# Regrouping PSUM for batches three to eight: three double and two single banks, attention in four pieces, relus over two banks

## The chip, the cores and the metric

One core of one Trainium2 chip. The metric is the device time of one execution in microseconds, median of several runs; all runs told here were in the fast state or, where there was one run only, of unknown state. The length of one batch inside the trace is from the first matmul of its first layer to the same matmul of the next batch.

## The reference

```python
k_proj = einsum('ks,bhsd->bhkd', E, k); v_proj = einsum('ks,bhsd->bhkd', F, v)
attn = softmax(q @ k_proj^T / 8)                 # 8 batches, 8 heads, 1024 rows, 64 wide
x = (attn @ v_proj) as 8192 x 512
out = relu(x @ w_in)**2 @ w_out                  # 512 -> 2048 -> 512
```

## The kernel before

Each batch has two chunks of 512 rows. A chunk is a first layer (16 groups of four 128x512 matmuls, emptied by relu on ScalarE and squared on VectorE) and a second layer (seven products by Strassen's scheme instead of eight, accumulated in ps_x, ps_y and ps_z). First-layer groups go in pairs: pair k has two halves, n = 0 and 1, that share one buffer of relus and are squared together. From the second batch on, steps are numbered 0 to 61: 0-15 and 31-46 are first-layer groups, 16-30 and 47-61 parts of products. Attention of the next batch is slipped in ahead of numbered steps: scores (q times k_proj), their exponentials, the sums of these and their reciprocals, values (exponentials times v_proj), and normalize (values times reciprocals). "Project" makes k_proj and v_proj. FFN matmuls use TensorE as one array of 128 x 128 ("128*128" in a profile line), scores and values as smaller tiles ("64*64", "64*32"). One turn from FFN matmuls to attention and back is called an excursion below, and the 0.216 us of one 512-column matmul, or of a set of tiles that runs at once (four scores, eight values), a slot. The program orders each engine by hand.

```python
aps = ...tile_pool(name="aps", bufs=2, space=PSUM)   # attention: 2 buffers of two banks
fps = ...tile_pool(name="fps", bufs=4, space=PSUM)   # FFN: 4 single banks, in turn

PIECES = {                                           # attention of the next batch, by step
    1: "copy_kp", 2: "copy_vp", 4: "copy_v_down",
    20: "scores 0, scores 1, exponentials 0", 21: "exponentials 1",
    23: "sums 0, values 0 0, reciprocals 0", 25: "normalize 0 0",
    28: "scores 2, scores 3, exponentials 2", 29: "exponentials 3",
    47: "values 0 1, sums 1, reciprocals 1", 48: "normalize 0 1",
    53: "values 1 0, values 1 1", 54: "normalize 1 0", 55: "normalize 1 1",
}                                                    # and "project" of the batch after at 53

def square(k, n, ps):                                # pair k, half n
    ...
    nc.scalar.activation(r[:, n], ps[:], AF.Relu)    # one relu per bank of 512 columns
    ...                                              # after n == 1: hsq = r * r on VectorE

second = [p1a, p2a, p1b, p1c] + lohi(p5) + lohi(p6) + lohi(p3) + lohi(p7) + [p2b]
second += [p4_last] if last else lohi(p4)
# p1, p6, p7, p4 accumulate into ps_y (read out after each); p5, p3 into ps_z; p2 into ps_x
```

The softmax here doesn't subtract the row's maximum and nothing guards it: scores larger than these inputs give would overflow.

Of the kernel before, what the change touches and what calls it, by code (L numbers as in the profile page):

```python
# [8 lines left out]
P = 128  # L9
F32 = mybir.dt.float32  # L10
BF16 = mybir.dt.bfloat16
AF = mybir.ActivationFunctionType
# [8 lines left out]
def kernel(  # L21
# [42 lines left out]
    sum_pool = ctx.enter_context(tc.tile_pool(name="sums", bufs=1))  # L64
    part_pool = ctx.enter_context(tc.tile_pool(name="part", bufs=1))
    out_pool = ctx.enter_context(tc.tile_pool(name="outp", bufs=2))
    aps = ctx.enter_context(tc.tile_pool(name="aps", bufs=2, space=bass.MemoryType.PSUM))
    fps = ctx.enter_context(tc.tile_pool(name="fps", bufs=4, space=bass.MemoryType.PSUM))

    def att_psum(shape, dtype):  # L70
        return aps.tile(shape, dtype, tag="att", name="ps_att")

    def ffn_psum(name, shape=(P, 512), dtype=F32):
        return fps.tile(list(shape), dtype, tag="ffn", name=name)

    def rows(src, b):
        return src[b].rearrange("h (p i) d -> p h (i d)", i=NI)
# [83 lines left out]
    class Attention:  # L161
# [9 lines left out]
        def transpose_q(self):  # L171
            nc.sync.dma_start_transpose(out=self.qT[:], in_=self.Q[:].rearrange("p h c -> p (h c)"))

        def project(self):
            ps = self.ps["kv"] = ffn_psum("ps_kv")
            kv = self.K[:].rearrange("p h (i d) -> p h i d", i=NI)
            vv = self.V[:].rearrange("p h (i d) -> p h i d", i=NI)
            for i in range(NI):
                f, l = i == 0, i == NI - 1
                nc.tensor.matmul(ps[0:KP, :], lhsT=ET[:, i, :], rhs=kv[:, :, i, :], start=f, stop=l)  # L180
                nc.tensor.matmul(ps[KP:P, :], lhsT=FT[:, i, :], rhs=vv[:, :, i, :], start=f, stop=l)  # L181
# [10 lines left out]
        def copy_vp(self):  # L192
            self.vp = proj_pool.tile([P, H, 2, D // 2], BF16, name="vp")
            ps = self.ps["kv"]
            ps_v = ps[KP:P, :].rearrange("k (h d e) -> k h e d", h=H, e=2)
            for e in range(2):
                nc.scalar.copy(self.vp[KP:P, :, e], ps_v[:, :, e])
# [209 lines left out]


    PIECES = {
        1: "copy_kp", 2: "copy_vp", 4: "copy_v_down",  # L410
        20: "scores 0, scores 1, exponentials 0", 21: "exponentials 1",
        23: "sums 0, values 0 0, reciprocals 0", 25: "normalize 0 0",
        28: "scores 2, scores 3, exponentials 2", 29: "exponentials 3",
        47: "values 0 1, sums 1, reciprocals 1", 48: "normalize 0 1",
        53: "values 1 0, values 1 1", 54: "normalize 1 0", 55: "normalize 1 1",
    }
    BATCH_1 = {
        33: "project", 34: "copy_kp, transpose_q, copy_vp", 37: "copy_v_down",
        48: "scores 0, scores 1, exponentials 0", 49: "exponentials 1",
        51: "scores 2, scores 3, exponentials 2", 52: "exponentials 3",  # L420
        55: "sums 0, sums 1, logs 0, logs 1, inverses 0", 57: "inverses 1",
# [2 lines left out]
    }  # L424

    BATCH_2 = {
        12: "project", 13: "copy_kp, transpose_q", 14: "copy_vp", 17: "copy_v_down",
        24: "scores 0, scores 1, exponentials 0", 25: "exponentials 1",
        27: "scores 2, scores 3, exponentials 2", 28: "exponentials 3",
        30: "sums 0, sums 1, logs 0", 31: "logs 1", 33: "inverses 0",  # L430
# [20 lines left out]
    def calls(table, n):  # L451
        for c in filter(None, table.get(n, "").split(", ")):
            name, *args = c.split()
            yield name, [int(a) for a in args]

    def ffn_groups(b, xT):
# [30 lines left out]
        def chunk(ch):  # L487
# [17 lines left out]
            def square(k, n, ps):  # L505
                hsq = st["hsq"]
                if n == 0:
                    st["r"] = relu_pool.tile([P, 2, TCH], F32, name="h_relu")
                r = st["r"]
                if (b, ch, k, n) == (0, 0, 0, 1):  # L510
                    nc.vector.tensor_scalar_max(r[:, n], ps[:], 0.0)
                else:
                    nc.scalar.activation(r[:, n], ps[:], AF.Relu)  # L513
                if n == 0:
                    return
                (h, j), (h1, _) = pairs[k]
                o = hsq[:, :, j, :] if h != h1 else hsq[:, h, j:j + 2, :]
                if k in ON_SCALAR.get((b, ch), ()):
                    nc.scalar.activation(o, r[:], AF.Square)
                    return operands_after(k)  # L520
                multiply = lambda: nc.vector.tensor_tensor(out=o, in0=r[:], in1=r[:], op=ALU.mult)  # L521
                if b == 0 and ch == 0 and k in (4, HFB - 1):
                    held.append(multiply)
                    return
                multiply()
                operands_after(k)
# [8 lines left out]
            def operands(q4, which):  # L535
                sums(st["hsq"], st["s"], q4, which)

            def step1(k, n):
                if k == 0 and n == 0:
                    begin()  # L540
                if held:
                    held.pop()()
                h, j = pairs[k][n]
                ps = ffn_psum("ps_h")
                first(ch, HFB * h + j, ps, range(NCB))
                square(k, n, ps)

# [25 lines left out]

            lo, hi = range(0, 4), range(4, 8)

            ALL = slice(0, 2)

            def bank(name):


                if last and name == "ps_y":
                    return [aps.tile([P, MH], F32, tag="att", name=name)[:] for _ in range(2)]
                return [ffn_psum(name)[:].rearrange("p (t m) -> p t m", t=2)]

            def parts(ps):

                return [(ps[0], ALL)] if len(ps) == 1 else [(ps[t], t) for t in range(2)]

            def copy(to, name):
                for ps, t in parts(st[name]):  # L590
                    nc.scalar.copy(to[:, t], ps)  # L591

            def add(to, name, more):
                for ps, t in parts(st[name]):
                    nc.vector.tensor_tensor(out=to[:, t], in0=ps, in1=more[:, t], op=ALU.add)  # L595

            def p1a():
                st["x"], st["y"], st["z"] = (bank(n) for n in ("ps_x", "ps_y", "ps_z"))
                h = st["hsq"]
                st["A11"], st["A12"] = h[:, 0, :, 0:TH], h[:, 1, :, 0:TH]  # L600
                st["A22"] = h[:, 1, :, TH:TCH]
                st["o0"], st["o1"] = (out_pool.tile([P, 2, DM], F32, name="o_sb") for _ in range(2))
                product(st["y"], st["A11"], W11, lo, True)

            def p2a():
                if b:
                    operands(1, (1, 3, 2))
                product(st["x"], st["A12"], W21, lo, True)

            def p1b():  # L610
                product(st["y"], st["A11"], W11, range(4, 7))
# [4 lines left out]
                copy(st["a"], "y")  # L616

            def p5(js):
                product(st["z"], st["s"][0], T1[:], js, js[0] == 0)
                if js[0]:  # L620
                    st["d"] = part_pool.tile([P, 2, MH], F32, name="p_d")
                    copy(st["d"], "z")
# [7 lines left out]
            def p3(js):  # L630
                product(st["z"], st["s"][3], W22, js)
                if js[0]:
                    add(st["o0"][:, :, MH:DM], "z", st["b"])
                    if last:
                        nc.sync.dma_start(out_rows[b, ch, 0, :, :, MH:DM], st["o0"][:, :, MH:DM])

            def p7(js):
                product(st["y"], st["s"][2], T3[:], js)
# [3 lines left out]
                        nc.sync.dma_start(out_rows[b, ch, 1, :, :, MH:DM], st["o1"][:, :, MH:DM])  # L642

            def p2b():
                product(st["x"], st["A12"], W21, hi)
                add(st["o0"][:, :, 0:MH], "x", st["a"])
                s = slice(0, MH if last else DM)
                nc.sync.dma_start(out_rows[b, ch, 0, :, :, s], st["o0"][:, :, s])

            def p4(js):  # L650
                product(st["y"], st["A22"], T4[:], js)
# [8 lines left out]
                    nc.sync.dma_start(out_rows[b, ch, 1, :, tb, 0:MH], st["o1"][:, tb, 0:MH])  # L660

            lohi = lambda p: [lambda: p(lo), lambda: p(hi)]
            second = [p1a, p2a, p1b, p1c] + lohi(p5) + lohi(p6) + lohi(p3) + lohi(p7) + [p2b]
            second += [p4_last] if last else lohi(p4)
            return steps, second, begin_sums, operands

# [20 lines left out]
    with tc.manual_schedule(engines=ORDERED):  # L687
# [11 lines left out]
        for b in range(B):  # L699
            for n, g in enumerate(ffn_groups(b, cur.xT)):  # L700
                if b == 0:
                    for name, args in calls(SECOND_HALF, n):
                        getattr(cur, name)(*args)
                    for name, args in calls(WEIGHTS, n):
                        combine_weights(args[0], name)
                    if n == 31:
                        nxt = load_batch(1)
                if nxt:
                    for name, args in calls((BATCH_1, BATCH_2, PIECES)[min(b, 2)], n):
                        getattr(nxt, name)(*args)  # L710
                    if n == (35, 14, 1)[min(b, 2)]:
                        ahead = load_batch(b + 2)
                    if b and n == 33 and ahead:
                        ahead.transpose_q()
                    if b and n == 53 and ahead:
                        ahead.project()
                g()
            if b == 0:
                nxt.normalize(1, 1)
            cur, nxt, ahead = nxt, ahead, None  # L720


# [28 lines left out]
```

## Time and profile before

| | before |
|---|---|
| median of 3 runs | 483.76 us (483.60 to 484.57) |
| span of the profiled run | 482.4 us |
| TensorE / VectorE / ScalarE busy | 470.3 / 314.1 / 261.5 us |
| a middle batch (third to sixth) | 57.30 us |
| the seventh batch (no projection) | 55.46 us |

### The profile page before, as it was taken

The page shows a single profiled execution, that of the slowest core. Times are in us where ns is not written, and L with a number is a line of the kernel's source. Part 1 is how long each engine was busy: PE and PEld are TensorE (multiplying, and loading weights), DVE is VectorE, ACT ScalarE, POOL GpSimd, SP SyncE. Part 2 cuts the span into 40 slices and gives each one's busy share as a digit, 9 for nine tenths or more (in the row PEclk, how much of TensorE's full clock was granted, in tenths as well). Part 3 has the DMA queues.
Part 4 walks back from the last instruction along what each step waited for, and adds up shares of the span by engine and source line. Part 5 has one row for each costly group of instructions (what it writes and reads, how often), then busy time and mean ns, then how long its engine had stood idle before and what let it go on. Part 6 is the DMA issues. An engine that isn't in the chain of part 4 may idle for free.

```text
span 482.4 us, 8423 instructions
## 1 busy us (share of the span) xinstructions
PE 470.3 (97%) x3630; PEld 292.6 (61%) x3630; DVE 314.1 (65%) x382; ACT 261.5 (54%) x413; POOL 34.7 (7%) x48
## 2 busy tenths in 40 slices
PE   4899999999999999999999999999999999999997
PEld 2544676475574746657475665747557474666656
DVE  1478955554958559493776848667494855948383
ACT  2387544758427564466635667176662756545351
POOL 6540020020020001000010000100000000000000
PEclk9999999999999999999999999999999999999999
DMA  9999989579989086941859147690702102020202
GB/s 155 203 204 207 168 181 200 137 120 229 180 128 229 12 175 88 180 94 50 153 86 227 22 115 131 91 200 1 165 11 75 25 1 88 1 88 0 88 1 87
DMA packets 72789, 55.46 MB, mean 115 GB/s; under 512 B 33968, under 2 KB 64944, under 8 KB 72752
## 3 DMA queue, kind: packets, MB, share of 16 engines
q0 software_dynamic: 30624, 29.36, 39.4%
q1 hardware_dynamic: 42128, 25.56, 21.1%
q8 instruction: 28, 0.46, 0.4%
q14 instruction: 9, 0.07, 0.0%
HBM read 59.24 MB, written 16.78 MB: 158 GB/s over the span
## 4 chain that ended last, share of the span: by engine, by line
PE 92%; DVE 3%; DMA 3%; ACT 1%; POOL 1%; issue 0%; POOLq 0%
PE ps_h L459 44%; PE ps_y L479 23%; PE ps_z L479 11%; PE ps_x L479 6%; DMA V_sb<-in_v_dram 3%; PE ps_kv L180 2%; PE ps_att L221 2%; PE ps_att L206 2%; DVE hsq L521 1%; DVE s L473 1%; PE ps_v L284 0%; DVE xT L246 0%; DVE xT L351 0%; PE ps_kv L181 0%; ACT h_relu L513 0%; POOL K_sb L93 0%
## 5 line engine op out<-in xcount | busy, mean ns | idle before, releaser
L459 PE MATMUL ps_h<-xT,w_in 128*128 128x512 bf16 x1024 | 224.8, 379 | 0.2 <-DVE xT L351 0.2
L521 DVE TENSOR_TENSOR hsq<-h_relu 128x1024 bf16<-128x1024 f32 x123 | 149.9, 1222 | 75.0 <-ACT h_relu L513 74.2
L513 ACT ACTIVATE h_relu<-ps_h 128x512 f32<-128x512 f32 x255 | 149.4, 597 | 63.4 <-PE ps_h L459 63.0
L459 PEld LDWEIGHTS <-w_in 128*128 128x128 bf16 x1024 | 99.7, 98 | 117.7 <-issue 1.9
L479 PEld LDWEIGHTS <-s 128*128 128x128 bf16 x1024 | 98.5, 98 | 19.8 <-issue 8.7
L479 PEld LDWEIGHTS <-hsq 128*128 128x128 bf16 x768 | 73.8, 98 | 17.3 <-issue 3.8
L479 PE MATMUL ps_y<-T,s 128*128 128x256 bf16 x512 | 62.4, 273 | 0.0
L246 DVE TENSOR_TENSOR xT<-ps_att,rs 128x1024 bf16<-128x1024 f32 x28 | 33.4, 1215 | 17.6 <-ACT rs L236 17.0
L473 DVE TENSOR_TENSOR s<-hsq 128x1024 bf16<-128x1024 bf16 x64 | 43.5, 683 | 0.0
L591 ACT COPY o_sb<-ps_y 128x512 f32<-128x512 f32 x15 | 8.8, 586 | 53.8 <-PE ps_y L479 53.7
L213 ACT ACTIVATE expT<-ps_att 128x1024 bf16<-128x1024 f32 x28 | 27.2, 1025 | 14.0 <-PE ps_att L206 14.0
L479 PE MATMUL ps_x<-w_out,hsq 128*128 128x256 bf16 x256 | 33.2, 273 | 0.0
L479 PE MATMUL ps_y<-w_out,hsq 128*128 128x256 bf16 x256 | 33.2, 273 | 0.0
L595 DVE TENSOR_TENSOR o_sb<-ps_z,p_b 128x512 f32<-128x512 f32 x16 | 11.0, 688 | 33.8 <-issue 19.9
L479 PE MATMUL ps_y<-T,hsq 128*128 128x256 bf16 x256 | 30.9, 272 | 0.0
L479 PE MATMUL ps_z<-T,s 128*128 128x256 bf16 x256 | 30.6, 273 | 0.0
L479 PE MATMUL ps_z<-w_out,s 128*128 128x256 bf16 x256 | 30.6, 273 | 0.0
L591 ACT COPY p_b<-ps_y 128x512 f32<-128x512 f32 (+1 forms) x17 | 9.4, 556 | 25.9 <-PE ps_y L479 25.8
L81 POOL DMA_DIRECT2D Q_sb<-in_q_dram x7 | 6.1, 876 | 227.7 <-DMA qT<-Q_sb 227.2
L473 DVE TENSOR_TENSOR s<-s,hsq 128x1024 bf16<-128x1024 bf16 x32 | 21.8, 684 | 0.3
L473 DVE TENSOR_TENSOR s<-hsq,s 128x1024 bf16<-128x1024 bf16 x32 | 21.7, 682 | 0.0
L591 ACT COPY p_a<-ps_y 128x512 f32<-128x512 f32 (+1 forms) x17 | 9.4, 561 | 21.8 <-PE ps_y L479 21.6
(75 smaller groups left out, 233.0 us busy)
## 6 DMA issues: line engine op xcount, KB each, us to landing
out_dram<-o_sb SPq DMA_DIRECT2D x30, 512.0 KB, 3.8
K_sb<-in_k_dram POOLq DMA_DIRECT2D x7, 1024.0 KB, 15.3
V_sb<-in_v_dram POOLq DMA_DIRECT2D x7, 1024.0 KB, 22.4
Q_sb<-in_q_dram POOLq DMA_DIRECT2D x7, 1024.0 KB, 9.4
w_out<-in_moe_w_out_dram POOLq DMA_DIRECT2D x4, 512.0 KB, 13.2
w_in<-in_moe_w_in_dram POOLq DMA_DIRECT2D x7, 256.0 KB, 10.0
K_sb<-in_k_dram POOLq DMA_DIRECT2D x2, 512.0 KB, 8.5
out_dram<-o_sb SPq DMA_DIRECT2D x3, 256.0 KB, 2.1
```

The costliest lines, as they stand in the source:

```text
L180: nc.tensor.matmul(ps[0:KP, :], lhsT=ET[:, i, :], rhs=kv[:, :, i, :], start=f, stop=l)
L206: nc.tensor.matmul(ps[o, bank, :], lhsT=self.kT[r, 2 * pr + j, :], start=True, stop=True, rhs=self.qT[r, NT * (2 * pr + j):NT * (2 * pr + ...
L213: nc.scalar.activation(e[:], self.ps["s", pr][:], AF.Exp, scale=SCALE)
L221: nc.tensor.matmul(ps[32 * j:32 * j + 32, a, :], lhsT=weights(o, 4 * g + j), rhs=self.exp[2 * g + j // 2][o, bank, :], start=True, stop=Tr ...
L246: nc.vector.tensor_tensor(out=self.xT[:, 2 * g + e].rearrange("p a n t -> p a (n t)"), in0=self.ps["v", g, e][:], in1=self.rs[g][:], op=AL ...
L459: nc.tensor.matmul(ps[:], lhsT=w_in_blk(cb, fb), rhs=xT[:, cb, :, 2 * ch:2 * ch + 2], start=(cb == 0), stop=(cb == NCB - 1),)
L473: nc.vector.tensor_tensor(out=s[o][:, js], in0=x, in1=y, op=op)
L479: nc.tensor.matmul(ps[tb] if len(ps) == 2 else ps[0][:, tb], lhsT=lhs[:, j, tb * P:(tb + 1) * P], rhs=rhs[:, j], start=first and n == 0 an ...
L513: nc.scalar.activation(r[:, n], ps[:], AF.Relu)
L521: multiply = lambda: nc.vector.tensor_tensor(out=o, in0=r[:], in1=r[:], op=ALU.mult)
L591: nc.scalar.copy(to[:, t], ps)
L595: nc.vector.tensor_tensor(out=to[:, t], in0=ps, in1=more[:, t], op=ALU.add)
```

## The change

The intent: fewer changes of TensorE between FFN and attention from the third batch on. Four pieces need three double-bank buffers, so the FFN gives up two of its four single banks; to make do, the even pairs of the first layer borrow the attention's double banks (one relu over both), ps_z shares its bank with ps_x, and single banks are handed out by their last use instead of in turn. The diff, cut to its core (left out, among more: the last batch has an order of products of its own, and keeps ps_x and ps_z apart):

```diff
+    att_pools = [aps (2 double)] * 2;  ffn_pools = [2 singles] + mixed [2 singles]
+    def regroup_psum():            # after the second batch: the mixed singles become one double
+        mixed_stack.close(); ...; att_pools.append(psum_pool("mps", 1))
+    def used(name):                # an evacuation moves its bank to the end of the list
+        ...
     PIECES = {
-        20: ..., 23: ..., 28: ..., 47: ..., 53: ...
+        18: "scores 0, scores 1, scores 2", 20: "exponentials 0, exponentials 1", 21: "exponentials 2",
+        23: "scores 3, exponentials 3",
+        27: "sums 0, sums 1, values 0 0, reciprocals 0", 28: "reciprocals 1", 29: "normalize 0 0",
+        49: "values 0 1, values 1 0, values 1 1", 51: "normalize 0 1", 53: "normalize 1 0",
+        55: "normalize 1 1",
     }
+    AHEAD = {23: "project", 24: "copy_kp", 25: "copy_vp", 26: "copy_v_down", 33: "transpose_q"}
...
-                else:
+                elif b < 2 or k % 2:
                     nc.scalar.activation(r[:, n], ps[:], AF.Relu)
+                elif n == 1:
+                    nc.scalar.activation(r[:], st["h"][:], AF.Relu)
...
-                ps = ffn_psum("ps_h")
+                if b < 2 or k % 2:
+                    ps = ffn_psum("ps_h")
+                else:
+                    if n == 0:
+                        st["h"] = att_psum([P, 2, TCH], F32)
+                    ps = st["h"][:, n]
...
+            before = lo if b == B - 1 else range(3 if b == 1 else 2)
-                product(st["x"], st["A12"], W21, lo, True)
+                product(st["x"], st["A12"], W21, before, True)
...
+                    st["z"] = st["x"] if 1 < b < B - 1 else bank("ps_z")
...
+            elif b > 1:
+                second = [p1a, p2a, p1b, p1c, p2b] + lohi(p6) + lohi(p5) + lohi(p7) + lohi(p3)
```

## The prediction

> **What bounds the kernel now.** I read the page's engine totals first, then TensorE's own waits, then one window per batch, then the timeline at the places that the change touches.
>
> ```profile
> PE 470.3 (97%) x3630; PEld 292.6 (61%) x3630; DVE 314.1 (65%) x382; ACT 261.5 (54%) x413; POOL 34.7 (7%) x48
> ```
>
> TensorE has matmuls in flight 97% of the span, VectorE and ScalarE have a third or more to spare. The list of TensorE's waits holds six entries, all from before 22 us, the largest 5.0 us for the first weights. So the usual question, which wait ends last, has the answer "none" for the batches that the change rewrites (third to eighth, from 142 us on). One window per batch says how long TensorE needs:
>
> ```profile
> 199.40:256.70 57.30, 57.30 (x433) 35.55 (x432) 38.61 (x45) 32.14 (x50) 2.62 (x3) 1.00 0.59 113
> 371.30:426.80 55.50, 55.50 (x418) 34.74 (x416) 37.74 (x43) 32.13 (x50) 0.00 (x0) 1.00 0.12 42
> 426.80:479.00 52.20, 52.12 (x352) 34.22 (x350) 33.18 (x39) 24.45 (x44) 0.00 (x0) 1.00 0.14 51
> ```
>
> Columns: stretch, length, busy us of matmul, weight load, VectorE, ScalarE, GpSimd. The last batch carries no attention for a later one: 52.20. The chain of waits gives 64 first-layer matmuls in 13.81 us (0.2158 each) and 8 second-layer ones in 0.873 us (0.109 each); 128 and 224 of them are 27.62 + 24.44 = 52.06 us. So a normal batch pays 57.30 - 52.20 = 5.10 us for attention and next to nothing for waiting. Only fewer or better packed TensorE instructions can shorten it. The timeline shows how attention is paid for:
>
> ```profile
> 214.79 1.04 PE L479 MATMUL ps_y<-w_out,hsq 128*128 128x256 bf16 x8
> 215.76 0.63 PE L206 MATMUL ps_att<-qT,kT 64*64 64x512 bf16 x8
> 216.32 1.92 PE L479 MATMUL ps_z<-T,s 128*128 128x256 bf16 x16
> ...
> 244.35 1.91 PE L479 MATMUL ps_z<-T,s 128*128 128x256 bf16 x16
> 246.19 0.63 PE L221 MATMUL ps_att<-expT,vp 64*32 64x512 bf16 x16
> 246.75 0.40 PE L180 MATMUL ps_kv<-K_sb,ET 128*64 128x512 bf16 x1
> ...
> 248.60 1.92 PE L479 MATMUL ps_y<-T,s 128*128 128x256 bf16 x16
> ```
>
> Eight second-layer matmuls need 0.87, yet 0.97 us pass from 214.79 to 215.76, and 0.56 more until the next product. The eight score matmuls are two slots of 0.216 (four 64x64 tiles at a time): 0.43 of work, so 0.97 + 0.56 - 0.87 - 0.43 = 0.23 us are lost on the excursion; the others give 0.22. The long excursion (values, then projection) takes 248.60 - 244.35 - 1.75 = 2.50 us for 0.43 + 1.73 of work: 0.34, so a second change of tile form inside an excursion costs 0.12. Before: four excursions of 0.65 and one of 2.50 = 5.10 us, which closes the account.
>
> **What the skill says.** "TensorEngine Tiling (Array Packing)", Tiling Modes, Key Properties: changing the tiling mode drains TensorE. The 0.22 us per excursion agrees. "TensorE: Matmul & The Clock Gate", "Wait — 56ns, not 53.3ns?": 215.7 ns between 512-column matmuls; here 215.8, so those cannot be made faster by scheduling. "ScalarE: Activation LUTs", What ACT_TABLE_LOAD costs: an ACTIVATE with immediate operands takes 186 ns + 0.833 per column, and neighbours overlap by 93 ns. The trace agrees closely: 597 ns for 512 columns, 1025 for 1024. "Perfetto Trace Analysis", Optimizing Scalar/DVE Operations: larger operations help if the engine is saturated. ScalarE is busy 32 of 57 us, so it is not.
>
> **The change, part by part.**
>
> *Double-bank relus.* Each pair with even index becomes one 1024-column relu instead of two of 512:
>
> ```profile
> L513 ACT ACTIVATE h_relu<-ps_h 128x512 f32<-128x512 f32 x255 | 149.4, 597 | 63.4 <-PE ps_h L459 63.0
> ...
> L213 ACT ACTIVATE expT<-ps_att 128x1024 bf16<-128x1024 f32 x28 | 27.2, 1025 | 14.0 <-PE ps_att L206 14.0
> ```
>
> 4 pairs x 12 chunks = 48 times 2 x 0.597 - 1.025 = 0.169: ScalarE loses 8.1 us of work, none on the path, so worth 0. But the relu can begin only when both halves are there, and its pair is complete 1.025 - 0.597 = 0.43 us later than before.
>
> *Attention in four pieces.* Three scores (3 slots, 0.65 + 0.22 = 0.87 us); one score and the projection (0.22 + 1.73 + 0.34 = 2.29); two sums and one value (0.87); three values (0.87): 4.90 us against 5.10. Without a projection, in the seventh batch: 0.87 x 3 + 0.44 = 3.05 against 5 x 0.65 = 3.25. One excursion fewer, 0.2 us, in five batches: **-1.0 us**.
>
> *Order of products.* The product on ps_x now ends before the others, and the last accumulation into ps_y follows ps_z instead of ps_x. That removes a small delay that the wait list doesn't name:
>
> ```profile
> 253.85 1.04 PE L479 MATMUL ps_x<-w_out,hsq 128*128 128x256 bf16 x8
> 254.05 0.69 DVE L595 TENSOR_TENSOR o_sb<-ps_y,p_d 128x512 f32<-128x512 f32 x1 [1.00 <-PE ps_y L479]
> 254.79 1.91 PE L479 MATMUL ps_y<-T,hsq 128*128 128x256 bf16 x16
> ```
>
> The add ends at 254.74, the matmul starts 0.05 later, at 254.79; free running would be 253.85 + 0.87 = 254.72. So 0.07 in the second chunk of each of six batches, **-0.4 us**, and VectorE's release costs TensorE 0.05.
>
> *Two single banks.* This is the price. The first product now needs the bank of the pair's last-but-one first-layer group:
>
> ```profile
> 211.52 0.60 ACT L513 ACTIVATE h_relu<-ps_h 128x512 f32<-128x512 f32 x1 [0.27 <-PE ps_h L459]
> 212.18 1.22 DVE L521 TENSOR_TENSOR hsq<-h_relu 128x1024 bf16<-128x1024 f32 x1
> 212.38 0.60 ACT L513 ACTIVATE h_relu<-ps_h 128x512 f32<-128x512 f32 x1 [0.27 <-PE ps_h L459]
> 213.05 1.04 PE L479 MATMUL ps_y<-w_out,hsq 128*128 128x256 bf16 x8
> 213.25 0.60 ACT L513 ACTIVATE h_relu<-ps_h 128x512 f32<-128x512 f32 x1 [0.27 <-PE ps_h L459]
> 213.92 1.22 DVE L521 TENSOR_TENSOR hsq<-h_relu 128x1024 bf16<-128x1024 f32 x1
> ```
>
> Take 213.05 as zero. A relu starts 0.20 after its group ends. The double relu of pair 6 starts at -1.53, where the single one does now, and its neighbour follows 0.93 later (1.025 less the overlap): -0.60, ending 0.00; with 0.05 for the release the first product starts at about +0.05. Eleven chunks of this kind (the last uses other banks): **+0.5 us**.
>
> *ps_z and ps_x in one bank* (batches three to seven): the product that opens ps_z waits for the add that empties ps_x. Estimate for the second chunk, from zero: the double relu delays VectorE, so pair 7's square runs 1.32 to 2.54 (0.87 to 2.09 now); with the operand instructions 0.60 apart, 0.71 for a dependent one, "normalize 0 1" starts at 4.38 and the add at 5.51, ending 6.20, so the bank is free at 6.25. TensorE arrives at 0.87 + 0.44 + 0.87 + 0.65 + 0.22 + 1.31 + 1.75 + 0.05 = 6.16. A wait of 0.1, five times: **+0.5 us**. In the first chunk no normalize stands before the add, and the bank is free at about 5.3: no wait. Pair 7's square (2.54) is needed at about 2.88: no wait either.
>
> *First two batches.* The shorter opening of ps_x moves 0.4 us of work behind the other products. In the first batch this removes two waits for ps_y (about 0.3) but lets scores 2 and 3 arrive before their exponentials release a buffer (about 0.25). In the second, the values at 131.3 already wait 0.26 us for a normalize, and TensorE comes 0.2 earlier. I put the sum at **0**.
>
> Total: -1.0 - 0.4 + 0.5 + 0.5 = -0.4 us, or 483.4 us.
>
> **Rivals.** (a) *All waits absent*: the pieces and the order are well placed, the release estimates are too late by a tenth; then -1.4 us, 482.3. For it: the distances are tiny, and the splits of the ps_x product look chosen to hit them. (b) *PSUM becomes the bound*: two single banks between first layer, products and VectorE's queue. VectorE is busy 38.6 of 57.3 us but is back to back at the end of each first layer, so each 0.3 us of error there is 0.3 us x 12 chunks = 3.6 us: 487. Against it: except for the two places above every release in my timing is 0.3 us or more early. (c) *Transfers*: the projection moves from step 53 to 23, which halves the time for K and V. In the third batch their loads are issued at 134-136 us and the DMA's traffic dies at about 158; the projection comes at about 162. Later batches have some 20 us more. If the third batch waits it is once, by 2 us at most: 485.5. (d) *ScalarE's 8 us return*: needs ScalarE on the path; the chain of waits gives ACT 1%. Not believed.
>
> **Range and chances.** The best case is bounded by what the account holds: 1.4 us, so 482; the measured runs spread over 1 us; errors in waits add upwards. Predicted 483.3, taking a little of rival (a); range 482.0 to 485.2. Two per cent is 9.7 us, 0.8 us per chunk: no part reaches it. Faster 0.01, within 2% 0.97, slower 0.02.
>
> **What would show it.** The window of a batch at about 57.2 us with no more than some 0.15 of waiting per chunk; four attention groups per batch, each with 0.22 us around it; waits of TensorE for the relu at the head of a chunk's products and for the add before ps_z opens, each 0.05 to 0.1; ScalarE some 8 us less busy at the same span. Wrong would be: batches under 56.9 us (a cost of matmuls that I don't see), a wait of 0.3 us or more that recurs in every chunk, or a projection that waits for V.

## The result, and the profile after

| | before | after |
|---|---|---|
| median | 483.84 us (483.49 to 485.30, 6 runs) | 483.81 us (482.96 to 484.78, 6 runs) |
| ratio | 1 | 0.9993 (95%: 0.9975 to 1.0011) |
| span of the profiled run | 482.4 us | 482.0 us |
| a middle batch | 57.30 us | 57.15 us |
| the seventh batch | 55.46 us | 55.30 us |
| third batch to the end of the last matmul | 336.99 us | 336.16 us |

A ratio is the mean time of one kernel's runs over that of the other's runs of the same rounds, so it is not quite the ratio of the medians. 483.81 lies in the predicted range. The last row is from the matmul timelines: 478.92 - 141.93 and 478.59 - 142.43.

The page's totals of the changed kernel, against the line that opens the prediction:

```profile
PE 469.5 (97%) x3630; PEld 293.7 (61%) x3630; DVE 314.8 (65%) x382; ACT 246.9 (51%) x365; POOL 34.4 (7%) x48
```

ScalarE is 14.6 us less busy, TensorE 0.8: the saving is nearly all on an engine that had time to spare. The groups of relus (instructions | busy us, mean ns):

```profile
L543 ACT ACTIVATE h_relu<-ps_h 128x512 f32<-128x512 f32 x159 | 92.4, 596 | 24.3 <-PE ps_h L489 24.1
...
L545 ACT ACTIVATE h_relu<-ps_att 128x1024 f32<-128x1024 f32 x48 | 49.1, 1023 | 55.2 <-PE ps_att L489 55.2
```

92.4 + 49.1 = 141.5 against 149.4 us: the durations save 7.9, as predicted. The rest of the 14.6 is overlap: a double relu is followed at once by its neighbour, and stretches in which two instructions overlap count once in the total.

Two middle batches, in the columns of the prediction's windows:

```profile
142.43:199.57 57.14, 57.14 (x434) 35.79 (x432) 38.71 (x45) 29.72 (x42) 2.63 (x3) 1.00 0.80 152
199.57:256.72 57.15, 57.15 (x434) 35.82 (x432) 38.72 (x45) 29.71 (x42) 2.63 (x3) 1.00 0.56 113
```

The third batch is as long as the fourth, so the projection, which now stands at 162.8 us in it, did not wait for V. The pieces in TensorE's timeline of the fourth batch, first chunk:

```profile
214.29 0.60 PE L509 MATMUL ps_z<-w_out,hsq 128*128 128x256 bf16 x4
214.82 0.84 PE L234 MATMUL ps_att<-qT,kT 64*64 64x512 bf16 x12
215.60 1.05 PE L509 MATMUL ps_y<-w_out,hsq 128*128 128x256 bf16 x8
...
217.79 1.91 PE L509 MATMUL ps_y<-T,s 128*128 128x256 bf16 x16
219.63 0.41 PE L234 MATMUL ps_att<-qT,kT 64*64 64x512 bf16 x4
...
221.82 1.92 PE L509 MATMUL ps_z<-T,s 128*128 128x256 bf16 x16
```

Three scores cost 215.60 - 214.29 less 0.44 for the four products = 0.87 us, score 3 with the projection 221.82 - 217.79 - 1.75 = 2.28, as worked out. And here is the price, the head of the second chunk's products:

```profile
241.78 1.89 PE L489 MATMUL ps_h<-xT,w_in 128*128 128x512 bf16 x8
241.98 1.02 ACT L545 ACTIVATE h_relu<-ps_att 128x1024 f32<-128x1024 f32 x1 [1.13 <-PE ps_att L489]
...
242.90 0.59 ACT L543 ACTIVATE h_relu<-ps_h 128x512 f32<-128x512 f32 x1
...
243.54 1.03 PE L509 MATMUL ps_y<-w_out,hsq 128*128 128x256 bf16 x8
```

The double relu holds its neighbour until 242.90; that ends at 243.49 and the product begins at 243.54, where free running would have been 241.78 + 1.73 = 243.51: 0.03 us lost. Six us later:

```profile
247.87 1.22 DVE L274 TENSOR_TENSOR xT<-ps_att,rs 128x1024 bf16<-128x1024 f32 x1
247.91 1.91 PE L509 MATMUL ps_y<-T,s 128*128 128x256 bf16 x16
249.00 0.68 DVE L639 TENSOR_TENSOR o_sb<-ps_z,p_a 128x512 f32<-128x512 f32 x1
...
249.74 1.91 PE L509 MATMUL ps_z<-T,s 128*128 128x256 bf16 x16
```

VectorE's add, behind a normalize, empties the shared bank at 249.68. TensorE, free at 247.91 + 1.745 = 249.655, begins at 249.74: 0.085 us lost. Neither wait is in the list of TensorE's waits, whose shortest entries are 0.2 us. Of what is new in that list, two entries belong to the start, before 22 us (0.5 and 0.2 us), and one to the second batch, which the change touches only at its edge:

```profile
PE ps_att L249 <- DVE xT L274: 0.3, 1, 0.3
```

Where the rest went that the batches gained (0.83) beyond the spans' difference (0.4): the second batch took 59.78 us instead of 59.60, and the first first-layer matmul started at 21.05 us in the profile before and at 21.43 after. Over the twelve profiles of the two kernels and the experiments it lay between 20.1 and 23.0 us. (In the profile after, for one, TensorE waited 0.5 us for the first load of K, which it did not before.)

### The profile page after: what moved, and what is told of

Same layout as the page of the kernel before. It is cut to its first block, busy times and chain, and to the rows that moved or that the text cites. A ratio compares the mean times of both kernels' runs of the same rounds, so it can differ in the third digit from the quotient of the medians.

```text
span 482.0 us, 8401 instructions
## 1 busy us (share of the span) xinstructions
PE 469.5 (97%) x3630; PEld 293.7 (61%) x3630; DVE 314.8 (65%) x382; ACT 246.9 (51%) x365; POOL 34.4 (7%) x48
## 2 busy tenths in 40 slices
DMA packets 72789, 55.46 MB, mean 115 GB/s; under 512 B 33968, under 2 KB 64944, under 8 KB 72752
## 4 chain that ended last, share of the span: by engine, by line
PE 91%; DVE 4%; ACT 2%; DMA 2%; issue 0%; ACTq 0%; POOLq 0%
PE ps_h L489 27%; PE ps_y L509 21%; PE ps_att L489 17%; PE ps_z L509 15%; PE ps_att L509 2%; PE ps_att L249 2%; DMA K_sb<-in_k_dram 2%; PE ps_att L234 2%; PE ps_att L207 2%; DVE hsq L553 1%; PE ps_x L509 1%; DVE s L503 1%; PE ps_kv L207 1%; ACT h_relu L543 1%; PE ps_k L290 1%; DVE xT L274 0%
## 5 line engine op out<-in xcount | busy, mean ns | idle before, releaser
L489 PE MATMUL ps_h<-xT,w_in 128*128 128x512 bf16 x640 | 147.8, 379 | 0.2 <-DVE xT L379 0.2
L543 ACT ACTIVATE h_relu<-ps_h 128x512 f32<-128x512 f32 x159 | 92.4, 596 | 24.3 <-PE ps_h L489 24.1
L489 PE MATMUL ps_att<-xT,w_in 128*128 128x512 bf16 x384 | 90.7, 379 | 0.0
L545 ACT ACTIVATE h_relu<-ps_att 128x1024 f32<-128x1024 f32 x48 | 49.1, 1023 | 55.2 <-PE ps_att L489 55.2
L509 PE MATMUL ps_y<-T,s 128*128 128x256 bf16 x480 | 57.7, 273 | 0.1
L509 PE MATMUL ps_y<-w_out,hsq 128*128 128x256 bf16 x240 | 31.2, 273 | 0.0
L509 PE MATMUL ps_y<-T,hsq 128*128 128x256 bf16 x240 | 29.0, 273 | 0.0
L633 ACT COPY p_a<-ps_y 128x512 f32<-128x512 f32 x15 | 8.8, 587 | 32.1 <-PE ps_y L509 32.1
```

What stands on the lines that cost most here:

```text
L489: nc.tensor.matmul(ps[:], lhsT=w_in_blk(cb, fb), rhs=xT[:, cb, :, 2 * ch:2 * ch + 2], start=(cb == 0), stop=(cb == NCB - 1),)
L509: nc.tensor.matmul(ps[tb] if len(ps) == 2 else ps[0][:, tb], lhsT=lhs[:, j, tb * P:(tb + 1) * P], rhs=rhs[:, j], start=first and n == 0 an ...
L545: nc.scalar.activation(r[:], st["h"][:], AF.Relu)
L633: nc.scalar.copy(to[:, t], ps)
```

## The experiments

All are correct. The fourth batch's length, from the matmul timelines (start of the fourth and fifth batch's first layer):

| run | fourth batch from, to (us) | length | time, ratio to before (95%) |
|---|---|---|---|
| before | 199.24, 256.54 | 57.30 | 483.84 us |
| after | 199.57, 256.72 | 57.15 | 483.81 us, 0.9993 |
| e1_single_relus | 206.66, 270.55 | 63.89 | 524.69 us, 1.0821 (1.0796 to 1.0847) |
| e2_order_only | 200.86, 258.10 | 57.24 | 484.81 us, 1.0001 (0.9976 to 1.0025) |
| e3_five_pieces | 200.46, 257.85 | 57.39 | 485.66 us, one run |
| e4_normalize_later | 199.10, 256.17 | 57.07 | 483.06 us, one run |
| e5_odd_pairs_double | 199.50, 256.60 | 57.10 | 483.93 us, one run |
| e7_two_relus_at_end | 198.98, 256.25 | 57.27 | 483.82 us, one run |
| e8_halves_apart | 198.68, 255.68 | 57.00 | 482.42 us, 0.9958 (0.9941 to 0.9976) |
| e6_all_three | 198.13, 255.13 | 57.00 | 482.74 us, 0.9968 (0.9949 to 0.9987) |
| e9_apart_and_early | 198.79, 255.79 | 57.00 | 482.90 us, 0.9973 (0.9956 to 0.9990) |
| e10_changed_again | 198.46, 255.61 | 57.15 | 483.25 us, 0.9989 (0.9970 to 1.0009) |

**e10_changed_again**: the changed kernel unedited, to know how far a batch length may be trusted.

> The changed kernel itself, unedited, once more on the same chip and in the same call as the combination, for a fair comparison and as a check of how well a batch repeats. Theory: middle batches 57.15 again to within 0.02, second batch 59.78, whole time within 0.3% of the kernel before, below it by 0.1 to 0.2%. Rival (batch lengths vary from run to run by as much as the differences that I read): 57.0 to 57.3.

57.15 again to the hundredth, and the second batch 59.78 again, as in every one of the eight profiles that leave it as the change made it. Batch lengths can carry differences of 0.05; whole times, whose 95% interval is 0.4% (2 us) wide, cannot.

**e1_single_relus**, on the changed kernel:

```diff
-                elif n == 1:
-                    nc.scalar.activation(r[:], st["h"][:], AF.Relu)
+                else:
+                    nc.scalar.activation(r[:, n], ps, AF.Relu)
```

> The changed kernel with one part undone: the even pairs keep their double bank, but are emptied by two relus of 512 columns again. Theory (TensorE's own instructions set the time, ScalarE has slack, and the double relu only makes releases later): ScalarE gets some 8 us busier, and a middle batch falls from 57.14 to about 57.0 us, because the waits at the head of the products (0.03 twice) and before ps_z opens in the second chunk (0.085) go; about 0.8 us in all, which the whole time hardly shows. Rival (the merged relus are what pays for the change): a batch grows by up to 8 x 0.169 = 1.35 us, 5 to 8 us in all.

Both were wrong: 40 us slower. The edit made a new wait. From TensorE's wait list, then the timeline:

```profile
PE ps_att L489 <- ACT h_relu L545: 33.7, 48, 0.7
```

```profile
206.66 1.03 PE L489 MATMUL ps_att<-xT,w_in 128*128 128x512 bf16 x4
...
207.79 0.60 ACT L545 ACTIVATE h_relu<-ps_att 128x512 f32<-128x512 f32 x1 [0.34 <-PE ps_att L489]
208.44 1.02 PE L489 MATMUL ps_att<-xT,w_in 128*128 128x512 bf16 x4 [0.74 <-ACT h_relu L545]
```

The second half's matmuls begin only when the first half's relu has ended (208.39), 208.44 - (206.66 + 0.86) = 0.92 us after they could have. A batch with eight such pairs is 63.89 - 57.15 = 6.74 us longer, 0.84 for each; 48 pairs are 40 us, the whole loss. The two halves lie in different banks and don't overlap, yet the wait is there. This program's synchronisation thus treats the two-bank buffer as one; that the chip itself would need it was not tested. So inside a shared two-bank buffer the double relu isn't a saving but a necessity, and the expectation had overlooked it. Two cleaner ways of undoing the relu follow.

**e7_two_relus_at_end**: two relus, both after the second half.

```diff
-                    nc.scalar.activation(r[:], st["h"][:], AF.Relu)
+                    for m in range(2):
+                        nc.scalar.activation(r[:, m], st["h"][:, m], AF.Relu)
```

> The changed kernel with the merge of the relus alone undone: both halves of the double bank are emptied by two relus of 512 columns, the second right behind the first, after the second half is written, so no matmul waits between the halves (which is what cost 40 us in the first experiment). Theory: the two end some 0.08 us later than the merged one, so the waits at the head of the products and before ps_z grow by 0.08 each: a middle batch of 57.15 becomes 57.3 to 57.4, and ScalarE is about 8 us busier. Rival (ScalarE's time counts as such): 57.15 + 8 x 0.17 = 58.5.

57.27: 0.12 longer, just under the 0.15 to 0.25 that was expected, and far from the rival's 1.35. The waits at the two heads grew from 0.04 to 0.10 us each (matmul starts, less the slots before them); the one before ps_z stayed at 0.08, against the expectation. ScalarE's busy total, 250.1 us, grew by 3.2 only, because of the overlap told above. Against two relus at the end, then, the merged relu is worth its earlier end, not its engine's time.

**e8_halves_apart**: each half of an even pair gets a double-bank buffer of its own, half of it unused, and its own relu at once.

```diff
-                    if n == 0:
-                        st["h"] = att_psum([P, 2, TCH], F32)
-                    ps = st["h"][:, n]
+                    ps = att_psum([P, TCH], F32)
```
(and the relu as in e1)

> The changed kernel with the double relus undone in the way that the first experiment meant it: each half of an even pair takes a double bank of its own (half of it unused) and is emptied at once by a relu of 512 columns. Theory: relus of even pairs end 0.43 us earlier, so both the wait at the head of the products (0.03 twice) and the one before ps_z (0.08) go: a middle batch of 57.15 becomes about 57.00 us, although ScalarE is 8 us busier. Rival (ScalarE's time or the lost half banks count): 57.3 or more.

57.00, as the theory said, in this window of the batch:

```profile
198.68:255.68 57.00, 57.00 (x434) 35.84 (x432) 38.73 (x45) 31.96 (x50) 2.63 (x3) 1.00 0.57 114
```

ScalarE is 2.2 us busier per batch than after, and the batch is 0.15 shorter. Of the matmuls that follow one of 128x128, only the four that begin an excursion start more than 0.02 us late in this batch: both waits are gone. So the double-bank relu, done to save ScalarE's time, costs TensorE 0.15 us per batch through its late end.

**e4_normalize_later**: which of the two waits is which.

```diff
-        49: "values 0 1, values 1 0, values 1 1", 51: "normalize 0 1", 53: "normalize 1 0",
+        49: "values 0 1, values 1 0, values 1 1", 52: "normalize 0 1", 53: "normalize 1 0",
```

> The changed kernel with the normalize of the second piece one step later, so that VectorE does the add that empties ps_x before it. Theory: the wait before ps_z opens in the second chunk goes, 0.085 us: a middle batch of 57.14 becomes about 57.06, and nothing else moves. Rival (the 0.085 is no wait for the add but the price of a first matmul into a bank, or of the weights): 57.14 as before.

57.07, so 0.08 less. The add now comes in time, and ps_z opens exactly 1.75 after the sixteen products before it:

```profile
247.43 1.91 PE L509 MATMUL ps_y<-T,s 128*128 128x256 bf16 x16
247.69 0.69 DVE L639 TENSOR_TENSOR o_sb<-ps_z,p_a 128x512 f32<-128x512 f32 x1 [0.21 <-PE ps_z L509]
...
249.18 1.04 PE L509 MATMUL ps_z<-T,s 128*128 128x256 bf16 x8
```

**e5_odd_pairs_double**: the parity of the pairs swapped, `k % 2` to `k % 2 == 0` in the two places of the diff.

> The changed kernel with double banks for the odd pairs and single banks for the even ones, so that the bank that the first product takes was emptied a pair earlier. Theory: the 0.03 at the head of both chunks' products goes and nothing else moves, because VectorE is behind by then whichever relu comes last: a middle batch of 57.15 becomes 57.08 to 57.09. Rival (pair 7's square, now 0.43 later, becomes the wait at the last part of the first product): 57.2 to 57.4.

57.10: 0.05 of the expected 0.06 to 0.07. The waits at the heads are gone, and the one before ps_z grew from 0.08 to 0.10. But its last chunk took 26.60 us (452.10 to 478.70) against 26.21 (452.38 to 478.59): there the third double bank goes to ps_x, and a late double relu has to empty it first. The combination e6 shows the same (below).

**e3_five_pieces**: one excursion more.

```diff
-        27: "sums 0, sums 1, values 0 0, reciprocals 0", 28: "reciprocals 1",
+        27: "sums 0, sums 1, reciprocals 0", 28: "values 0 0, reciprocals 1",
```

> The changed kernel with the third piece cut in two at a place without waits near it (value 0 0 goes one step later than the two sums). Theory: one excursion more, 0.22 us in each of the five batches that carry attention: a middle batch of 57.14 becomes 57.36. Rival (an excursion costs nothing by itself, the 0.22 is the work of its slots or the wait for its data): no change, 57.14.

57.39, 0.24 more with the same matmuls. The timeline:

```profile
226.31 0.62 PE L249 MATMUL ps_att<-expT,ones 64*32 64x512 bf16 x16
226.87 1.05 PE L509 MATMUL ps_z<-w_out,s 128*128 128x256 bf16 x8
227.84 0.41 PE L249 MATMUL ps_att<-expT,vp 64*32 64x512 bf16 x8
228.19 1.05 PE L509 MATMUL ps_z<-w_out,s 128*128 128x256 bf16 x8
```

The lone value takes 228.19 - 226.87 - 0.87 = 0.45 us for one slot of 0.216: 0.23 is the excursion, the same that every excursion of the kernel before showed, and no wait is recorded ahead of it. The rival falls. A change of product and bank within the 128x128 form costs nothing (in e4, ps_z opens exactly 1.75 us after sixteen matmuls into ps_y); so the price goes with the change of tile form, though no run splits it further.

**e2_order_only**, on the kernel before: the new order of products from the third batch on, old banks, pieces and relus (in the last batch, too, where the changed kernel has an order of its own).

```diff
+            if b > 1:
+                second = [p1a, p2a, p1b, p1c, p2b] + lohi(p6) + lohi(p5) + lohi(p7) + lohi(p3)
             second += [p4_last] if last else lohi(p4)
```
(and the store of the first output rows moved to where they are complete)

> The kernel before with one part of the change alone: from the third batch on the order of products of the changed kernel (ps_x finished before ps_y goes on, ps_z between the last two accumulations into ps_y), but the old banks, pieces and relus. Theory: only the wait of the last accumulation into ps_y goes, 0.07 to 0.09 us in each second chunk: a middle batch of 57.31 us becomes about 57.23, the last of 52.16 about 52.05, 0.5 us in all. Rival (the gain of the change comes from the order, not from the pieces): 57.15 or less.

57.24: 0.06 to 0.07 of the 0.15 comes from the order. The delay before the last accumulation into ps_y is gone from the matmul starts. The rest is the pieces' gain less the new waits: e2 and e8, neither with a wait left in this batch, have five excursions and four, and differ by 57.24 - 57.00 = 0.24, the same as e3; less the 0.15 of waits that e8 takes out, 0.09 remains.

**e6_all_three**: e4 and e5 together, and the opening of ps_x in the first two batches by chunk:

```diff
-            before = lo if b == B - 1 else range(3 if b == 1 else 2)
+            before = lo if b == B - 1 or (b, ch) == (1, 1) else range(3 if (b, ch) in ((0, 1), (1, 0)) else 2)
```

> The changed kernel with the later normalize, the double banks on the odd pairs, and in the first two batches an opening of ps_x of four, three or two block columns by chunk, as each one's waits ask. Theory: a middle batch of 57.15 becomes 57.00 (0.08 and 0.07 less), the first two batches together lose 0.3 to 0.5 us; from the first product-feeding matmul to the end some 1.2 us less than the changed kernel and 2.0 less than the kernel before, about 0.3 to 0.4% of the whole time. Rival (the waits move to the next buffer): batches of 57.1 or more.

57.00 and 59.63 for the second batch (after: 59.78, before: 59.60), but the gain over the changed kernel from the first-layer matmul at 36.70 us (37.75 in the changed kernel) to the end of the last matmul was 0.6 us (440.25 against 440.84), not 1.2. The last chunk gave 0.4 back:

```profile
464.16 1.04 PE L509 MATMUL ps_att<-w_out,hsq 128*128 128x256 bf16 x8
464.36 1.02 ACT L545 ACTIVATE h_relu<-ps_att 128x1024 f32<-128x1024 f32 x1 [1.13 <-PE ps_att L489]
...
465.44 1.03 PE L509 MATMUL ps_att<-w_out,hsq 128*128 128x256 bf16 x8 [0.24 <-ACT h_relu L545]
```

The product on ps_x (465.44) waits for the double relu that ends at 465.38; free running would be 464.16 + 0.87 = 465.03.

**e9_apart_and_early**: e8 with the opening of e6.

> The kernel of halves_apart, with the opening of ps_x in the first two batches of four, three or two block columns by chunk (as in all_three). Theory: middle batches of 57.00 as there, the second batch 59.62 instead of 59.78 us, the last chunk 26.2 (not the 26.6 that all_three pays, where its third bank waits for a late double relu); whole time 0.3 to 0.5% under the kernel before and some 0.2 to 0.3% under the changed kernel of the same call. Rival (what is left is noise of the start): no difference to the changed kernel.

57.00, second batch 59.64, last chunk 26.20. From the second batch to the last matmul it needs 395.06 us (82.15 to 477.21), the changed kernel 395.96 (81.53 to 477.49), the kernel before 396.59 (82.33 to 478.92). In time it is 0.27% faster than before; against e10 the medians differ by 0.35 us and the runs overlap (482.11 to 483.68, 482.71 to 485.24), so that it beats the changed kernel is shown by the traces and not by the clock.

## Why the prediction was right

- **The bound.** TensorE's instruction stream, with next to no waits: right. Raising ScalarE's busy time in a batch by 2.2 us (e8) or 0.5 us (e7) moved the batch by 0.15 us or less, and in e8 the other way. Two readings of the prediction are loose: the 5.0 us put down to the first weights is the wait for E in bf16 (ps_E), and the last batch's window ends 0.08 us after the last matmul, so its 52.20 is 52.12 of matmuls and the account closes less exactly than it says.
- **The pieces, -1.0.** One excursion saved, at 0.22 us. e3 puts one back and pays 0.24, and e2 against e8 gives 0.24 again; the new pieces measure 0.87 and 2.28 in the trace.
- **The order, -0.4.** e2: 0.06 to 0.07 per batch, as read from the delay at 254.79.
- **Two single banks, +0.5.** The wait is where it was put, at 0.036 to 0.038 (matmul starts, less the slot before) instead of 0.05 in each of eleven chunks, so 0.4 us. e5 takes it out.
- **ps_z in ps_x's bank, +0.5.** Some 0.08 instead of 0.1, five times, so 0.4; only in the second chunk, as foreseen; e4 takes it out.
- **First two batches, 0.** Mis-sized. The second batch took 59.78 us instead of 59.60. The shorter opening of ps_x brings TensorE to the values earlier, where it waits for the same normalize; the delay before the second value grew from some 0.27 to 0.49 us:

```profile
131.44 0.41 PE L249 MATMUL ps_att<-expT,vp 64*32 64x512 bf16 x8
132.15 0.41 PE L249 MATMUL ps_att<-expT,vp 64*32 64x512 bf16 x8 [0.29 <-DVE xT L274]
```

  (132.15 - 131.44 less one slot of 0.216.) Restoring four block columns there (e9) gives 0.14 of it back.
- **Sum.** From the third batch on, -0.83 us measured against -0.4. The terms as measured, -1.2 for the five excursions saved, -0.4, +0.4 and +0.4, make -0.8, so none is missing; the saving per excursion (0.24, not 0.20) and the two waits were a little mis-sized. The whole time, 483.81, is 0.5 above the predicted 483.3, inside what the start varies by; e10's 483.25 shows the spread. The whole time therefore tests little: "no change" would have fitted it as well, and that it falls in the range is no evidence for a gain of 0.4. What bears the prediction out is the batch lengths and the waits in the traces; the gain from the third batch on was put 0.4 too low and the loss in the second batch 0.2 too low, and that these partly cancel is luck.
- **ScalarE "some 8 us less busy".** 7.9 as a sum of durations, but 14.6 on the page: overlap was not considered.
- **Rivals.** (a) describes e8 and e9, not the change itself. (b) fell: the tight banks cost 0.04 us in a first chunk and 0.12 in a second. (c) fell: the third batch is not longer than the fourth. (d) fell by e7 and e8.

## What to carry to other kernels

When one engine has work all the time, judge a change by that engine's instructions and by the releases that they wait for, and price each of its switches: an excursion cost 0.22 to 0.24 us here, and 0.12 more with a second tile form in it. A merged instruction on an engine with slack saved nothing here, and its later end cost the bound engine; ask when the release comes, not how long the engine is busy. Where differences are tenths of a per cent, compare a repeated stretch inside the traces rather than whole times.

## What the Trainium skill lacked or had wrong

- "TensorEngine Tiling (Array Packing)", Tiling Modes: says that a change of tiling mode drains TensorE, without a figure. The runs show 0.22 to 0.24 us for an excursion of 128x128 matmuls to a tiled form and back (e3: 57.39 against 57.15 us), and 0.12 for a second tiled form within it. That the drain is what takes this time was not tested.
- "ScalarE: Activation LUTs", What ACT_TABLE_LOAD costs: 186 ns + 0.833 per column would be 612 and 1039 ns; relus from PSUM took 596 and 1023 ns, 2 to 3% less. The page does not say which memory its instruction read.
- No page gives the time from the end of a ScalarE or VectorE instruction to the matmul that waits for it: 0.05 to 0.06 us (243.49 to 243.54, 249.68 to 249.74).
- No page warns that a program may synchronise a two-bank PSUM buffer as one, so that reading one bank holds up matmuls into the other: 0.84 us each time, 40 us in e1.
